# Attention and expert kernel on one core: third operands of the 320-column chunk dealt alike in all experts, attention steps handed out from a fixed list, three gate tiles

## The chip, the core and the metric

The kernel runs on one core of a Trainium2 chip. A core has five engines that run side by side, each working through its own queue in order: TensorE (PE in the profile; PEld are its weight loads), VectorE (DVE), ScalarE (ACT), GpSimd (POOL) and SyncE (SP), which here issues most of the transfers. They wait for each other by semaphores. Matmuls write to PSUM, the other operands lie in SBUF. The metric is the device time of one execution in microseconds (us). Three runs of the kernel before gave 425.80, 425.93 and 425.94, median 425.93.

## What is computed

Sketched attention gives `x`, and a mixture of four experts of width 1024 is applied to it, all in float32:

```python
a, b = x @ S1.T, x @ S2.T                    # phi(x): all 64 products a_i * b_j
kv, z = sum_s phi(k) v, sum_s phi(k)         # for each batch and head
x = (phi(q) @ kv) / (phi(q) @ z + 1e-6)      # 4 x 1088 rows of 4 * 32 = 128 columns
p = domain_probs / (domain_probs.sum(-1) + 1e-9)
out = sum over e of p[:, e] * (relu(x @ w1[e]) @ w2[e])    # e = 0..3, 128 -> 1024 -> 128
```

## The kernel before

The 4352 tokens lie along the columns and are cut into ten chunks (`CHUNKS`): 128, 448, six of 512, then 320 (chunk 8) and 384 (chunk 9). In each chunk but the first the four experts are worked through, each in eight blocks of 128 hidden units. A block is one slot of the main loop, 32 slots for each chunk. Attention for the later tokens is computed in between, in small steps from a generator (`pieces`).

A number is split into two or three parts of fewer bits, so that three fast passes of TensorE stand for one float32 product. A block has six matmuls, all recorded at L949:

- `h <- xs,wa` and `h <- xs,wb` when its slot opens (`opening`). ScalarE then scales h in place (`h <- h`, L1135).
- `h <- xs,wd` one slot later (`third`). Then the three operands of the second product are made from h: `ha`, the rounded high part of relu(h); `hb`, the rest (L1191, always VectorE); and `hc`, the operand of the third pass.
- `o <- ha,va` and `o <- hb,vb` five slots after the block opened (`LAG`, in `second`).
- `o <- hc,vd` only when the expert's eight blocks are through: ScalarE scales o (L1268), and `pay` hands the eight passes out over the next slots, 0, 1, 1, 2, 2, 2 (`DEALT`). Then the expert is gathered: VectorE multiplies o by the gate (L1396; L1394 for the first expert) and adds it to the total (L1397). The experts use two PSUM banks of o in turn, so the first o product of the next expert but one waits for this gather.

Who makes ha and hc is told by a letter for each block (`MAKERS`, a row of eight letters for each chunk and expert; the row of chunk 8 is the seventh). ScalarE's scaling of h and VectorE's hb are the same for all. The letters that matter here:

| letter | ScalarE | VectorE, besides hb | GpSimd |
|---|---|---|---|
| A | ha (L1184), hc (L1186) | - | hc = hb - hc (L1214) |
| P | ha | - | hc from ha (L1213), then L1214 |
| V | ha | hc from ha and hb (L1193) | - |
| D | hc | ha from h (L1188) | L1214 |
| N | ha, a "whole" from ha (L1197) | hc from h and the whole (L1206) | - |
| Z | ha | the whole (L1199), hc (L1206) | - |

L1193 has both operands in SBUF; L1188, L1191, L1199 and L1206 read h from PSUM. There are 7 tiles for ha, 6 for hb, 13 for hc, and six PSUM banks for h.

A gate is one expert's weight for each token of a chunk, repeated over all partitions: a tile of up to 512 columns, loaded by SyncE from a DRAM buffer (`load_gates`, L429). There are two tiles (`GATES`). The first two are loaded in slot 5, in front of the keys and values of batch 1 (`load_k(1)`, `load_v(1)`); each later one is issued behind a gather (`next_gates`) and takes the tile that this gather has just read. Loads that stand behind it in SyncE's queue wait with it.

How many attention steps follow a slot is decided while the program is built, by a planner: `on_vector` adds up an estimated time of what is issued to VectorE and ScalarE, `needed` and `left` say how many steps have to be done by when, and `work` hands out steps as credit and limits (`LIMIT`, `SLOT`, `LEAD`) allow. By the time of chunk 8 all but a few steps are done. In chunk 8 the other work besides the blocks is the gathers, the turning round of chunk 7's rows (L1362) and the splitting of chunk 9's tokens (`token_parts`: L886 on ScalarE, L891 on VectorE, L961 on GpSimd).

Of the kernel before, what the change touches and what calls it, by code (L numbers as in the profile page):

```python
# [24 lines left out]
def kernel(  # L25
# [24 lines left out]
    nc = tc.nc  # L50
# [4 lines left out]
    B, H, S, D = q.shape  # L55
# [10 lines left out]
    CW = 512  # L66
    GE = 160
    LAG = 5
    GATES = 2
    BUFFERS = (7, 6, 13)  # L70
    HA, HB, HC = BUFFERS
    WHOLE = 5
    MIXED = 16
    TURN = 1
    MAKER_1 = 'APXPDADA'
    MAKERS = (('APPVANAA', 'APAVPVAA', 'APPPAVAN', 'APVPAADA'), ('PAPPVBBA', 'APAVPAAA', 'APPVPANA', 'APVPADAA'), ('APPVNAAA', 'PAAVPAVA', 'AVPPPANA', 'APVPADAA'), ('APVAQNAA', 'APPVANPA', 'APVPAADA', 'APPVAAAD'), ('NPPVAPAN', 'APPAVAPA', 'NPPVAANP', 'APVPAADA'), ('APNVAPAA', 'APAPVAVA', 'APPVPANA', 'APVPDAAA'), ('APPVNAAZ', 'APAVVAAP', 'AAPVPPNA', 'APVPDAAA'), ('NVPVPAAV', 'PPVPVNPA', 'APVVPPDN', 'APvAAQaA'))
    TAIL = 4
    MAKER_TAIL = "PAVVXXTT"
    LAG_TAIL = 4
    DEALT_TAIL = (1, 1, 2)  # L80
    DEALT = (0, 1, 1, 2, 2, 2)
    LIMIT = 1300.0
    LIMIT_A = 1e9
    SLOT_A = 1500.0
    SLOT = 1600.0
    PLAIN = (2,)
    TOKENS_AT = 16
    AHEAD = 13
    TOKENS = 6
    LEAD = 6  # L90
    SETTLE = 1
    SPREAD = 2
    XD_BY = 'PPVVPPPVPP'
    Q_BY = 'PVPPPPVVPVVVPVVPPP'
    O_BY = 'AAAA'
    FETCH = 8
    HOLD = (3, 1)
    DELAY = 0
# [8 lines left out]
    UNITS = [[P, 448, 512], [576, 512], [576, 512], [576, 512]]  # L107

    CHUNKS = [P, 448] + [512] * 6 + [320, 384]
    NC = len(CHUNKS)  # L110
    START = [sum(CHUNKS[:m]) for m in range(NC + 1)]
# [34 lines left out]
    def load_k(b):  # L146
        kn[b] = lpool.tile([P, S], F32, tag="rows", name="kn")
        load_rows(k, b, kn[b])
# [266 lines left out]
    def parts(m):  # L415

        c, end, at = START[m], START[m] + CHUNKS[m], 0
        while c < end:
            n = min(end, (c // S + 1) * S) - c
            yield c // S, c % S, n, at  # L420
            c, at = c + n, at + n
# [3 lines left out]
    def load_gates(m, experts):  # L425
        for e in experts:
            gate[m, e] = mpool.tile([P, CW], F32, tag="gate", bufs=GATES, name="gate")
            for b, c, n, at in parts(m):
# [99 lines left out]
    def key_sum(b, p, kv, t0=0, n=NT):  # L528
        for t in range(t0, t0 + n):
            both(  # L530
                kv[:, 256 * p : 256 * p + 2 * (D + 1)],
                kps[b][:, t, p, :],
                vx[:, t, 2 * p : 2 * p + 2].rearrange("p h d -> p (h d)"),

                start=(p == t == 0),
                stop=(t == NT - 1),
                skip_group_check=True,
            )
# [275 lines left out]
    def queries_by_dram(b, c, n):  # L814

        for _ in range(FETCH):
            yield
# [7 lines left out]
        if c + n < S:  # L825
# [3 lines left out]
            if c + n + m == S and b < B - 1:  # L829
                load_k(b + 1)  # L830
        for _ in range(14 - FETCH):
            yield
# [133 lines left out]
    def start():  # L966
# [37 lines left out]
        for t0, n0 in ((0, 4), (4, 5)):  # L1004
            for p in range(2):
                key_sum(b, p, kv, t0, n0)
        qp = [xd_ for xd_ in (mpool.tile([P, CW], F32, tag="gate", bufs=GATES, name="qp") for _ in range(2))]
        for x in range(2):
# [40 lines left out]
    slots = [("pair", 0, e, f) for e in range(E) for f in range(NP)]  # L1049
    for m in range(1, NC):  # L1050
        slots += [("one" if m > 1 or FB * e + k >= MIXED else "mixed" if FB * e + k >= WHOLE else "whole", m, e, k) for e in range(E) for k in range(FB)]
    first_slot = {m: min(i for i, s in enumerate(slots) if s[1] == m) for m in range(NC)}
    per_chunk = {m: sum(s[1] == m for s in slots) for m in range(NC)}
# [23 lines left out]
    def final(m, e):  # L1077
        return m == NC - 1 and e == E - 1

    def letter(m, e, b):  # L1080
        if m == 1 and FB * e + b < MIXED:
            return "X"
        return (MAKER_TAIL if final(m, e) else MAKER_1 if m == 1 else MAKERS[m - 2][e])[b]

# [135 lines left out]
    def second(i):  # L1220
# [25 lines left out]
        elif kind == "one":  # L1246
# [19 lines left out]
            elif k == FB - 1:  # L1266
                if O_BY[e] == "A":
                    nc.scalar.activation(o[:, 0:n], o[:, 0:n], ACTF.Copy, scale=1.0 + R12)  # L1268
# [133 lines left out]
                yield  # L1402
            turn_back(m, total.pop(m)[:, 0:n])

    vector_time, scalar_time = [0.0], [0.0]

    def on_vector(inst):

        if inst.engine == mybir.EngineType.DVE and inst.outs:
            n = 1  # L1410
            for _, d in list(inst.outs[0].ap)[1:]:
                n *= d
            vector_time[0] += n / 0.96 + 80
        elif inst.engine == mybir.EngineType.Activation and inst.outs and type(inst).__name__ != "InstDMACopy":
            n = 1
            for _, d in list(inst.outs[0].ap)[1:]:
                n *= d
            scalar_time[0] += n * 0.834 + 50

    start()  # L1420
    nc.push_inst_callback(on_vector)
    pieces = front()
    done, credit = [0], [0]

    def piece():
        done[0] += 1
        next(pieces, None)


    needed, columns, count = [0] * NC, UNITS[0][0], 0  # L1430
    for b in range(B):
        count += 17 if b else 0
        for n in UNITS[b] if b else UNITS[0][1:]:
            count, columns = count + (20 if count else 18), columns + n
            for m in range(NC):
                if columns - n < START[m] + CHUNKS[m] <= columns:
                    needed[m] = count
    for i in range(3):
        begun_hp[i] = psum(ps_h, "h")
        half_columns(i, begun_hp[i], 0)  # L1440
# [25 lines left out]
        due.setdefault(first_slot[1] + HOLD[1] if held else i + (LAG_TAIL if final(*s[1:3]) else lag[s[0]]), []).append(i)  # L1466
    i = 0
    while i < len(slots) or i <= max(due) or owed:
        vector_time[0] = max(0.0, vector_time[0] - (SLOT * CHUNKS[slots[i][1]] / CW if i >= first_slot[1] and i < len(slots) else 900.0))
        scalar_time[0] = max(0.0, scalar_time[0] - (SLOT_A * CHUNKS[slots[i][1]] / CW if i >= first_slot[1] and i < len(slots) else 900.0))  # L1470
        if i < len(slots):
            kind, m, _, _ = slots[i]
            at = i - first_slot[m]
            while have[0] < START[m] + CHUNKS[m]:
                piece()

            gone = START[m] + CHUNKS[m] * at / per_chunk[m]
            left = lambda c: START[c] - (CHUNKS[c - 1] * AHEAD / per_chunk[c - 1] if c > 1 else 0) - gone
            rate = CHUNKS[m] / per_chunk[m] * max(
                [0] + [(needed[c] + (LEAD if c > 1 else 4) - done[0]) / left(c) for c in range(m + 1, NC) if left(c) > 0]  # L1480
            )

            def work(share):

                if not first_slot[1] <= i < first_slot[1] + 4:
                    credit[0] = min(credit[0] + rate * share, 3)
                while credit[0] >= 1 and vector_time[0] < LIMIT and scalar_time[0] < LIMIT_A:
                    credit[0] -= 1
                    piece()

            opening(i)
            if kind == "pair":
                work(0.5)
        for j in due.get(i, ()):
            second(j)
        if SETTLE:
            settle()
        third(i - DELAY if i < len(slots) else i)
        if not SETTLE:
            settle()  # L1500
        pay()
        next(ending, None)
        if i < len(slots):
            work(0.5 if kind == "pair" else 1)
            if at == per_chunk[m] - AHEAD and 0 < m < NC - 1:
                while have[0] < START[m + 1] + CHUNKS[m + 1]:
                    piece()
            for gen in to_part.get(i, ()):
                next(gen, None)
            if m == NC - 2 and at == per_chunk[m] // 2:  # L1510
                while have[0] < B * S:
                    piece()
                w2_tail = load_tail()
                one = dram.tile([P, P], F32, name="one")
                nc.sync.dma_start(one[:, :], unit[:, 0:P])
                nc.sync.dma_start(bass.AP(one.tensor, one.offset, [[P + 1, P], [1, 1]]), unit[:, P : P + 1])
                nc.sync.dma_start(unit[:, 0:P], one[:, :])
            if i == first_slot[1] + 10:
                for j in range(3):
                    load_plain(j)  # L1520
            for j in range(3, len(plain_order)):
                if i == first_slot[2] + 8 * (j - 3) + 7:
                    load_plain(j)
            if i == first_slot[4]:
                unit = cpool.tile([P, P + 1], F32, tag="dp", name="unit")
                nc.gpsimd.memset(unit[:, 0:P], 0.0)
                nc.gpsimd.memset(unit[:, P : P + 1], 1.0)
            if i == 2:
                gate_quotients()
            elif i == 5:  # L1530
                store_gates()
                next_gates(GATES)
                load_k(1)
                load_v(1)
        if i == 2:

            made_hp[3] = psum(ps_h, "h")
            for c in (0, HP):
                half_columns(3, made_hp[3], c)
        i += 1  # L1540
    for _ in ending:
        pass
    last_rows(NC - 1, unit)
    nc.pop_inst_callback()

# [1 line left out]
_INS = ["q", "k", "v", "S1", "S2", "moe_domain_probs", "moe_w1", "moe_w2"]  # L1547
# [26 lines left out]
```

## Time and profile before

| | |
|---|---|
| median of three runs | 425.93 us |
| the profiled execution's own time | 426.43 us |
| its span, first to last instruction | 424.7 us |
| instructions | 8812 |
| granted TensorE clock | 1.0 over the whole span |
| first product of chunk 8 (128x320) | 353.29 us |
| first product of chunk 9 (128x384) | 383.68 us |
| gathers of chunk 7 in this stretch, experts 2 and 3, begin at | 357.31 and 365.15 us |
| gathers of chunk 8, experts 0 to 2, begin at | 372.25, 379.64 and 387.52 us |

The profile is a trace of one execution, with a page that sums it up. In lines of groups a line names the line of the kernel, the engine, the operation, what it writes and reads with the shape, and how often; behind that stand busy time, the mean of one in ns, and the idle time of the engine before it with what ended it. In lines of the timeline the first two numbers are start and length in us, in tables of windows each engine's busy time in that stretch. Neighbouring instructions of one engine can overlap in the records: their lengths say more than an engine needs for each, and the distance from start to start in a full stretch is its real pace.

### The profile page before, as it was taken

How to read it: one execution, taken by the hardware profiler on the slowest of the kernel's cores; microseconds unless marked ns; L12 is line 12 of the kernel's file. 1: busy time of each engine (PE TensorE's matmuls, PEld its weight loads, DVE VectorE, ACT ScalarE, POOL GpSimd, SP SyncE). 2: the span in 40 equal slices, each digit the busy share in tenths (PEclk: the TensorE clock that was granted, in tenths of full speed). 3: DMA queues.
4: the chain of work that ended last, by engine and by line, in shares of the span. 5: the costliest groups of instructions: out<-in, count | busy, mean ns of one | idle time of the engine just before them, and what ended most of it. 6: DMA issues, size and time to landing. Idle time of an engine off the chain costs nothing.

```text
span 424.7 us, 8812 instructions
## 1 busy us (share of the span) xinstructions
PE 416.5 (98%) x2819; PEld 351.7 (83%) x2819; DVE 357.0 (84%) x626; ACT 382.0 (90%) x818; POOL 355.3 (84%) x371
## 2 busy tenths in 40 slices
PE   9999999999999999999999999999999999999996
PEld 7886677888888887878888887878778888989995
DVE  5869999888798896898799996896897878879894
ACT  4368898999999998999999988998999999999992
POOL 6441468999999999997999998897989999799992
PEclk9999999999999999999999999999999999999999
DMA  6925250446512401643602415212621221040110
GB/s 194 320 60 130 47 145 2 98 80 158 165 40 51 126 27 44 136 99 95 176 5 61 114 26 117 61 33 62 161 32 23 41 75 35 23 82 27 34 38 19
DMA packets 57646, 34.66 MB, mean 82 GB/s; under 512 B 34945, under 2 KB 50689, under 8 KB 57601
## 3 DMA queue, kind: packets, MB, share of 16 engines
q1 hardware_dynamic: 57504, 34.01, 31.5%
q8 instruction: 22, 0.36, 0.4%
q14 instruction: 24, 0.19, 0.2%
q10 hardware_dynamic: 96, 0.10, 0.1%
HBM read 28.94 MB, written 5.15 MB: 80 GB/s over the span
## 4 chain that ended last, share of the span: by engine, by line
PE 82%; ACT 8%; DVE 4%; issue 3%; DMA 2%; SPq 0%; DVEq 0%; ACTq 0%
PE o L949 36%; PE h L949 36%; PE h L318 6%; ACT ha L1184 3%; ACT h L1135 3%; ACT hc L1186 2%; PE h L497 1%; DMA qn_first<-in_q_dram 1%; PE o L318 1%; DMA kn<-in_k_dram 1%; PE h L1121 1%; DVE hb L1191 1%; DVE o L1396 1%; SPq L171 0%; DVE qs L637 0%
## 5 line engine op out<-in xcount | busy, mean ns | idle before, releaser
L1214 POOL TENSOR_TENSOR hc<-hb,hc 128x512 fp32r<-128x512 f32 (+3 forms) x204 | 252.5, 1260 | 23.1 <-DVE hb L1191 16.9
L1191 DVE SCALAR_TENSOR_TENSOR hb<-h,ha 128x512 fp32r<-128x512 f32 (+3 forms) x266 | 166.8, 641 | 48.9 <-ACT hc L1186 16.9
L1135 ACT ACTIVATE h<-h 128x512 f32<-128x512 f32 (+3 forms) x283 | 166.3, 588 | 4.1 <-PE h L949 3.5
L1184 ACT ACTIVATE ha<-h 128x512 fp32r<-128x512 f32 (+3 forms) x252 | 148.8, 590 | 2.0 <-PE h L949 0.4
L949 PE MATMUL h<-xs,wd 128*128 128x512 f32 (+3 forms) x283 | 109.2, 386 | 1.3 <-ACT h L1135 0.5
L949 PE MATMUL h<-xs,wa 128*128 128x512 f32 (+3 forms) x283 | 105.5, 373 | 0.0
L949 PE MATMUL h<-xs,wb 128*128 128x512 f32 (+3 forms) x283 | 102.5, 362 | 0.0
L949 PE MATMUL o<-ha,va 128*128 128x512 f32 (+3 forms) x266 | 96.8, 364 | 1.1 <-DVE total L1397 1.1
L949 PE MATMUL o<-hb,vb 128*128 128x512 f32 (+3 forms) x266 | 96.6, 363 | 0.0
L949 PE MATMUL o<-hc,vd 128*128 128x512 f32 (+3 forms) x262 | 79.7, 366 | 0.2
L1186 ACT ACTIVATE hc<-h 128x512 fp32r<-128x512 f32 (+3 forms) x124 | 74.1, 598 | 0.0
L949 PEld LDWEIGHTS h<-xs,wd 128*128 128x128 f32 x283 | 53.3, 188 | 19.8 <-ACT h L1135 11.6
L1213 POOL TENSOR_SCALAR hc<-ha 128x512 fp32r<-128x512 f32 (+3 forms) x80 | 57.4, 717 | 8.1 <-ACT ha L1184 1.6
L949 PEld LDWEIGHTS h<-xs,wa 128*128 128x128 f32 x283 | 53.5, 189 | 9.5 <-issue 2.9
L949 PEld LDWEIGHTS h<-xs,wb 128*128 128x128 f32 x283 | 53.5, 189 | 5.7 <-issue 0.6
L949 PEld LDWEIGHTS o<-ha,va 128*128 128x128 f32 x266 | 50.3, 189 | 7.5 <-PE h L949 2.3
L949 PEld LDWEIGHTS o<-hc,vd 128*128 128x128 f32 x262 | 48.5, 189 | 7.9 <-issue 1.6
L949 PEld LDWEIGHTS o<-hb,vb 128*128 128x128 f32 x266 | 50.3, 189 | 5.5 <-DVE hb L1191 0.2
L1193 DVE SCALAR_TENSOR_TENSOR hc<-ha,hb 128x512 fp32r<-128x512 f32 (+2 forms) x41 | 36.2, 882 | 1.4
L1268 ACT ACTIVATE o<-o 128x512 f32<-128x512 f32 (+3 forms) x33 | 18.4, 557 | 0.0
L1397 DVE TENSOR_TENSOR total<-o,total 128x512 f32<-128x512 f32 (+3 forms) x26 | 16.9, 650 | 0.9
L1396 DVE TENSOR_TENSOR o<-o,gate 128x512 f32<-128x512 f32 (+3 forms) x26 | 16.8, 647 | 0.3 <-PE o L949 0.3
(161 smaller groups left out, 405.2 us busy)
## 6 DMA issues: line engine op xcount, KB each, us to landing
w_sb<-in_moe_w_dram SPq DMA_DIRECT2D x8, 512.0 KB
gate<-gates SPq DMA_DIRECT2D x16, 256.0 KB
kn<-in_k_dram SPq DMA_DIRECT2D x4, 544.0 KB
gate<-gates SPq DMA_DIRECT2D x8, 224.0 KB
qs<-rows SPq DMA_DIRECT2D x6, 288.0 KB
qs<-rows SPq DMA_DIRECT2D x12, 144.0 KB
qn<-in_q_dram SPq DMA_DIRECT2D x3, 544.0 KB
vx<-in_v_dram SPq DMA_DIRECT2D x48, 32.0 KB
```

Source lines behind the costliest of these rows:

```text
L318: nc.tensor.matmul(out(s), weights(s), moving(s), **flags)
L949: nc.tensor.matmul(to, weights, t, **flags)
L1135: nc.scalar.activation(g, g, ACTF.Copy, scale=1.0 + R12)
L1184: nc.scalar.activation(ha, g, ACTF.Relu, scale=NEAR)
L1186: nc.scalar.activation(hc, g, ACTF.Relu, scale=NEAR * R12)
L1191: nc.vector.scalar_tensor_tensor(out=hb, in0=g, scalar=0.0, in1=high, op0=ALU.max, op1=ALU.subtract)
L1193: nc.vector.scalar_tensor_tensor(out=hc, in0=high, scalar=-R12, in1=rest, op0=ALU.mult, op1=ALU.add)
L1213: nc.gpsimd.tensor_scalar(out=hc, in0=high, scalar1=R12, scalar2=1.0, op0=ALU.mult, op1=ALU.mult)
L1214: nc.gpsimd.tensor_tensor(out=hc, in0=rest, in1=both_, op=ALU.subtract)
L1268: nc.scalar.activation(o[:, 0:n], o[:, 0:n], ACTF.Copy, scale=1.0 + R12)
L1396: nc.vector.tensor_tensor(out=o[:, 0:n], in0=o[:, 0:n], in1=g, op=ALU.mult)
L1397: nc.vector.tensor_tensor(out=total[m][:, 0:n], in0=o[:, 0:n], in1=total[m][:, 0:n], op=ALU.add)
```

## The change

Three things change. The numbers of attention steps that follow each slot are written down as digits (`PIECES`), and the planner goes. `GATES` is 3 instead of 2. And the four rows of letters of chunk 8 become one pattern, APVDAPVD, for all four experts; counted over its 32 blocks, A 14, P 9, V 5, N 2, Z 1, D 1 become A 8, P 8, V 8, D 8.

```diff
-    GATES = 2
+    GATES = 3
...
     MAKERS = (
...
-      ('APPVNAAZ', 'APAVVAAP', 'AAPVPPNA', 'APVPDAAA'),
+      ('APVDAPVD', 'APVDAPVD', 'APVDAPVD', 'APVDAPVD'),
...
-    LIMIT = 1300.0
-    LIMIT_A = 1e9
-    SLOT_A = 1500.0
-    SLOT = 1600.0
...
-    LEAD = 6
...
+    PIECES = "0110110111011000301101101110110100001212121212111122002211111021210221112102211121110111110003011102111110002111111111111100301111..."
...
-            def work(share):
-
-                if not first_slot[1] <= i < first_slot[1] + 4:
-                    credit[0] = min(credit[0] + rate * share, 3)
-                while credit[0] >= 1 and vector_time[0] < LIMIT and scalar_time[0] < LIMIT_A:
-                    credit[0] -= 1
+            def work():
+
+                steps[0] += 1
+                for _ in range(int(PIECES[steps[0] - 1])):
                     piece()
...
             if kind == "pair":
-                work(0.5)
+                work()
...
-            work(0.5 if kind == "pair" else 1)
+            work()
```

`on_vector`, `needed`, `gone`, `left` and `rate`, which only the planner used, are taken out with it.

More of the change, by code (lines that the diff above doesn't have):

```diff
@@ L75 @@
     MAKER_1 = 'APXPDADA'
-    MAKERS = (('APPVANAA', 'APAVPVAA', 'APPPAVAN', 'APVPAADA'), ('PAPPVBBA', 'APAVPAAA', 'APPVPANA', 'APVPADAA'), ('APPVNAAA', 'PAAVPAVA', 'AVPPPANA', 'APVPADAA'), ('APVAQNAA', 'APPVANPA', 'APVPAADA', 'APPVAAAD'), ('NPPVAPAN', 'APPAVAPA', 'NPPVAANP', 'APVPAADA'), ('APNVAPAA', 'APAPVAVA', 'APPVPANA', 'APVPDAAA'), ('APPVNAAZ', 'APAVVAAP', 'AAPVPPNA', 'APVPDAAA'), ('NVPVPAAV', 'PPVPVNPA', 'APVVPPDN', 'APvAAQaA'))
+    MAKERS = (('APPVANAA', 'APAVPVAA', 'APPPAVAN', 'APVPAADA'), ('PAPPVBBA', 'APAVPAAA', 'APPVPANA', 'APVPADAA'), ('APPVNAAA', 'PAAVPAVA', 'AVPPPANA', 'APVPADAA'), ('APVAQNAA', 'APPVANPA', 'APVPAADA', 'APPVAAAD'), ('NPPVAPAN', 'APPAVAPA', 'NPPVAANP', 'APVPAADA'), ('APNVAPAA', 'APAPVAVA', 'APPVPANA', 'APVPDAAA'), ('APVDAPVD', 'APVDAPVD', 'APVDAPVD', 'APVDAPVD'), ('NVPVPAAV', 'PPVPVNPA', 'APVVPPDN', 'APvAAQaA'))
     TAIL = 4
@@ L95 @@
     O_BY = 'AAAA'
+    PIECES = "01101101110110003011011011101101000012121212121111220022111110212102211121022111211101111100030111021111100021111111111111003011110210211100301111021111110012111100210211002111111020111100121111021101110030111101201011000210110020101100201010100000000000000000000000000000000000000000000000000000000000000000000000000000"
     FETCH = 8
@@ L1403, in gather @@
             turn_back(m, total.pop(m)[:, 0:n])
[L1405 to L1418, printed above, removed]
     start()
-    nc.push_inst_callback(on_vector)
     pieces = front()
-    done, credit = [0], [0]
+    steps = [0]
     def piece():
-        done[0] += 1
         next(pieces, None)
[L1430 to L1437, printed above, removed]
     for i in range(3):
@@ L1468 @@
     while i < len(slots) or i <= max(due) or owed:
-        vector_time[0] = max(0.0, vector_time[0] - (SLOT * CHUNKS[slots[i][1]] / CW if i >= first_slot[1] and i < len(slots) else 900.0))
-        scalar_time[0] = max(0.0, scalar_time[0] - (SLOT_A * CHUNKS[slots[i][1]] / CW if i >= first_slot[1] and i < len(slots) else 900.0))
         if i < len(slots):
@@ L1475 @@
                 piece()
[L1477 to L1481, printed above, removed]
-            def work(share):
-                if not first_slot[1] <= i < first_slot[1] + 4:
-                    credit[0] = min(credit[0] + rate * share, 3)
-                while credit[0] >= 1 and vector_time[0] < LIMIT and scalar_time[0] < LIMIT_A:
-                    credit[0] -= 1
+            def work():
+                steps[0] += 1
+                for _ in range(int(PIECES[steps[0] - 1])):
                     piece()
@@ L1543 @@
     last_rows(NC - 1, unit)
-    nc.pop_inst_callback()
 _INS = ["q", "k", "v", "S1", "S2", "moe_domain_probs", "moe_w1", "moe_w2"]
```

## The prediction

> **What bounds the kernel now.** I read the page first: busy shares, then the chain that ended last.
>
> ```profile
> PE 416.5 (98%) x2819; PEld 351.7 (83%) x2819; DVE 357.0 (84%) x626; ACT 382.0 (90%) x818; POOL 355.3 (84%) x371
> ...
> PE 82%; ACT 8%; DVE 4%; issue 3%; DMA 2%; SPq 0%; DVEq 0%; ACTq 0%
> ```
>
> TensorE sets the end; the others can only cost the time in which it waits for them. So I went to the stage that the change touches. The chunk of 320 columns issues its first product at 353.29 and the last chunk (384 columns) starts at 383.68, so the stage is 30.4 us. I then took the busy time of each engine from 358.64 (the first hb behind the gather of chunk 7, expert 2) to 388.45 (the first VectorE instruction behind the gather of chunk 8, expert 2).
>
> ```profile
> 358.64:388.45 29.81, 29.12 (x192) 26.97 (x191) 25.47 (x53) 29.61 (x84) 25.91 (x34) 1.00 0.21 46
> ...
> 388.00:400.00 12.00, 12.00 (x77) 11.72 (x76) 11.41 (x23) 11.90 (x31) 10.92 (x13) 1.00 0.14 40
> ```
>
> After the length come PE, PEld, DVE, ACT, POOL. ScalarE is full (29.61 of 29.81), VectorE has 4.34 us free. (The second row, from the last chunk, is used below.) The busy time of PE hides its waits, so I read these from the starts of its matmuls:
>
> ```profile
> 366.08 0.30 PE L949 MATMUL h<-xs,wb 128*128 128x320 f32 x1
> 366.71 0.37 PE L949 MATMUL o<-ha,va 128*128 128x320 f32 x1 [0.33 <-DVE total L1397]
> ...
> 380.17 0.30 PE L949 MATMUL o<-hb,vb 128*128 128x320 f32 x1
> 380.61 0.40 PE L949 MATMUL h<-xs,wd 128*128 128x320 f32 x1
> ```
>
> Undisturbed 320-wide matmuls start 0.1355 us apart (360.46, 360.60, 360.74, 360.87); 366.08 to 366.71 is 0.63, so 0.49 is lost, and 380.17 to 380.61 loses 0.30. Summed over every start from 358.56 to 389.58 (steps 0.1355, 0.1625 and 0.2155 for 320, 384 and 512 columns), the gaps of 0.07 or more lose 3.04 us. Of this 0.25 lies at 358.87, behind a gather in front of which nothing changes, and 0.10 at 389.34, past the stretch. **At most 2.7 us can be had.** Apart from the 0.57 at 366.71, behind a VectorE gather, nearly all are at wd products waiting for ScalarE's h (L1135), or at hc products while ScalarE scales o (L1268). VectorE waits too:
>
> ```profile
> DVE hb L1191 <- ACT ha L1184: 1.2, 4, 0.6
> DVE hb L1191 <- PE h L949: 1.1, 2, 0.6
> DVE hb L1191 <- ACT hc L1186: 0.9, 2, 0.5
> DVE hb L1191 <- PE o L949: 0.6, 1, 0.6
> DVE hb L1191 <- POOL hc L1214: 0.2, 1, 0.2
> ```
>
> 4.0 us in all: idle because ScalarE, and TensorE behind it, were late.
>
> **The change, part by part.** *PIECES* holds the very counts that the planner arrives at in the kernel before, and the planner runs at build time. The order of TensorE's instructions is the same in both kernels, that of the others differs only in the chunk of 320 and, on SyncE, in the gate loads. Cost nothing.
>
> *GATES 3* puts one more gate load (224 KB) in front of the keys of batch 1 on SyncE: a gate issue takes 0.43 us (two took 0.86 at 33.08), the key load went out at 33.99 and is first read at 52.97, so 18.5 us hide it; without that cover it would cost its 0.43. Every later gate load still stands behind the gather whose tile it takes, so the loads queued behind it wait as before. No VectorE wait on a gate load is in the list of waits, so nothing is to be had either: zero, bounds 0 and 0.4. Each then brings the gate of one expert later than before, so gates come a whole expert sooner; the tightest was issued at 379.01 and used at 387.52, 8.5 us ahead.
>
> *Letters.* The 32 blocks of the chunk go from A14 P9 V5 N2 Z1 D1 to A8 P8 V8 D8. ScalarE: 7 ha and 2 "whole" fewer, one hc more, so 8 of its 80 block instructions go. Start to start in a full stretch (362.20 to 362.51, 361.88 to 362.20) hc costs 0.31 and ha 0.32; a whole waits for its own ha and costs 0.54. 6 x 0.32 + 2 x 0.54 = 3.0 us. 29.61 - 3.0 = 26.6, and TensorE without its waits would need 29.8 - 2.7 = 27.1: ScalarE stops being the limit, by little. GpSimd: one TENSOR_SCALAR less (0.54), the same 24 TENSOR_TENSOR; the first expert has six instead of five (+0.84), hidden since the first hc pass comes 13 slots after its block opens (361.1 made, 367.19 used); if that cover failed it is late by that 0.84.
>
> VectorE pays: V from 5 to 8, ha in D from 1 to 8, three hc of N and Z and one Z whole fewer.
>
> ```profile
> L1191 DVE SCALAR_TENSOR_TENSOR hb<-h,ha 128x320 fp32r<-128x320 f32 x31 | 14.4, 484 | 3.8 <-PE h L949 1.1 <-ACT ha L1184 1.0 <-ACT hc L1186 0.9
> L1193 DVE SCALAR_TENSOR_TENSOR hc<-ha,hb 128x320 fp32r<-128x320 f32 x5 | 3.6, 723 | 0.2
> ...
> L1188 DVE TENSOR_SCALAR ha<-h 128x320 fp32r<-128x320 f32 x1 | 0.5, 475 | 0.0
> ```
>
> Start to start: hb 0.41 (four in 1.73 at 384.52), ha 0.51 (384.01 to 384.52). The five hc of V took 0.41, 0.69, 0.41, 0.60 and 1.10 to the next start, mean 0.64, and the hb ahead of each 0.10 more than usual: 0.74. N's hc 0.41, Z's whole 0.52. So 3 x 0.74 + 7 x 0.51 - 3 x 0.41 - 0.52 = **+4.0 us on VectorE**, as much as the waits that it had.
>
> **The sum.** VectorE's queue is in order: behind a late V stand the next ha and hb (o products wait for both) and the gathers, and behind a gather the first o product of the next expert but one. The tightest is the gather of chunk 8, expert 2: it ends at 388.53 and TensorE takes its bank at 388.82; a hand-off took 0.14 at 366.71, so 0.15 is spare. If VectorE never idles it does the stretch in 25.5 + 4.0 = 29.5, plus the 0.3 of idle time that is no listed wait, 29.8: as before. By start-to-start prices alone its work was 31 hb 12.7, one 384-wide hb 0.5, five V 3.7, four hc of N and Z 1.7, a whole and an ha 1.0, four gathers 1.33 + 0.54 + 0.93 + 0.93, the turn of chunk 7's rows 0.62 and a token part 1.03: 25.0; it becomes 29.0, which is 0.8 sooner. TensorE gains the difference and the spare 0.15: between 0.15 and 0.95 us. I take 0.5, the middle, since both ends come from the same rows. The 2.2 that remain of 2.7 turn from waits for ScalarE into waits for VectorE. From 390 on TensorE runs full (the second row above), so the 0.5 reaches the end. On the profiled execution (426.43; span 424.7 and 1.73 around it) that is 425.9; its median stands 0.5 lower, 425.93, and so the forecast is **425.4**, own range 425.0 to 425.9. A measurement here tells 0.2%, 0.85 us, from no change, so this is no change.
>
> **What the hc of V really costs** decides more than anything else. The row first:
>
> ```profile
> 369.59 0.49 DVE L1193 SCALAR_TENSOR_TENSOR hc<-ha,hb 128x320 fp32r<-128x320 f32 x1
> ...
> 382.51 1.18 DVE L1193 SCALAR_TENSOR_TENSOR hc<-ha,hb 128x320 fp32r<-128x320 f32 x1
> ```
>
> At 369.59 GpSimd was idle; at 382.51 its TENSOR_TENSOR had begun 0.03 earlier and ran 0.86. hb, which reads h from PSUM, is steady at 0.484. So 0.41 and 1.10 are the bounds of one such step. The Trainium skill ("SBUF — State Buffer", section "SBUF: two separate sides") speaks against the change: a VectorE instruction with two SBUF inputs and a GpSimd one lock a shared port pair for a whole instruction, and the later one stands still. This trace agrees (1.18 is about the rest of 0.83 plus 0.35). A lock met at random would make the average hc dearer than the five rows do. By that the sum would be the second rival's, 426.6.
>
> **Rivals.** (1) *VectorE keeps up.* The regular deal puts hc into GpSimd's gaps and it costs 0.41 + 0.10 each: 8 x (0.74 - 0.51) = 1.8 us less, gain 0.5 + 1.8 = 2.3 of the possible 2.7: **423.6**. For: two of five cost 0.41, and VectorE ran 11.41 of 12.00 in 388 to 400 with no TensorE wait. Against: GpSimd is busy 25.9 of 29.8. (2) *Slower: GpSimd holds VectorE up.* GpSimd's four instructions per four blocks are three of 0.87 and one of 0.46; caught at random, the rest of one is (3 x 0.87 x 0.87 + 0.46 x 0.46) / (2 x 3.07) = 0.40, times the 95% that it is busy, 0.38; hc is 0.41 + 0.38 + 0.10 = 0.89 instead of 0.74, and 8 x 0.15 = 1.2 us late. That alone takes the 0.5 and 0.7 more, **426.6**; if all were caught as at 382.51 (1.20), 8 x 0.46 = 3.7 gives 429.1. It decides from 0.80 per V on. For: the two 384-wide ones at 389.03 and 390.74 lasted 0.74 and 1.07. Against: the five measured. (3) *It doesn't do what it says:* ScalarE is freed but the waits at 366.71 and at bank hand-overs stay put, as they are VectorE's: **425.9**.
>
> **Chances.** Forecast 0.34, rival 1 0.31, rival 2 0.25, rival 3 0.10. Faster by over 0.2%: rival 1 and the edge of the forecast, 0.33. Slower: rival 2, 0.25. Within: 0.42. The range takes in rival 1 and rival 2 at its first price: 423.6 to 427.0.
>
> **What would show it.** ScalarE's busy share in the stage drops by 3 us and PEld's waits for h L1135 vanish there; VectorE's share rises above 28 of the stage with hardly a wait for ScalarE; new TensorE waits name DVE total L1393 or hb. L1193's row (now L1189), x8 at 320: mean near 0.72 confirms the sum, under 0.6 rival 1, over 0.85 rival 2. The first 353 us must be the same to 0.2 us; if they are not, PIECES or GATES was priced wrongly, and so was the forecast.

## The result and the profile after

| | before | after |
|---|---|---|
| median of five runs each, same chip | 425.93 us | 427.78 us (427.64 to 428.20) |
| ratio, 95% interval | 1 | 1.0043 (1.0031 to 1.0055) |
| the profiled execution's own time, span | 426.43, 424.7 us | 427.78, 426.0 us |
| first product of chunk 8 to that of chunk 9 | 30.39 us | 30.84 us |
| first product of chunk 8 to that of the last block | 61.35 us | 62.71 us |

The change costs 1.85 us of the median; the forecast was a gain of 0.5. Here and below, ratios and intervals are estimated from the fast runs alone (one of the twelve runs of e10, 1101.73 us, is not in them), so a ratio can differ from the quotient of the two medians, by up to 0.0009. Lines behind the constants are four lower in the changed kernel (hb L1187, V's hc L1189, ha of D L1184, the gather L1392 and L1393).

The page of the changed kernel, busy time by engine and the chain that ended last:

```profile
PE 416.1 (98%) x2819; PEld 351.0 (82%) x2819; DVE 362.1 (85%) x632; ACT 380.4 (89%) x810; POOL 354.4 (83%) x370
...
PE 85%; ACT 5%; DVE 3%; issue 2%; DMA 2%; SPq 0%; ACTq 0%; DVEq 0%
```

TensorE does the same 2819 matmuls and still ends last; VectorE has 5.1 us more to do, ScalarE 1.6 less. The next rows are the stretch between the same two VectorE instructions as in the prediction (first hb behind the gather of chunk 7, expert 2, to the first behind that of chunk 8, expert 2) and 388 to 400, with the busy time of PE, PEld, DVE, ACT, POOL:

```profile
358.34:389.73 31.39, 30.09 (x194) 27.31 (x192) 29.82 (x60) 28.64 (x79) 27.29 (x35) 1.00 0.18 45
388.00:400.00 12.00, 11.49 (x72) 11.18 (x72) 11.57 (x23) 11.54 (x30) 9.41 (x12) 1.00 0.14 33
```

The stretch is 31.39 us instead of 29.81. ScalarE, which had 0.20 us free in it, now has 2.75. VectorE's 29.82 busy are what its whole old stretch lasted. And from 388 to 400, where TensorE had been full, it now idles for half a microsecond. Which engine waits for which from 358.34 to 390.20 (us in all, times, longest):

```profile
PE o L945 <- DVE total L1393: 0.9, 2, 0.5
...
DVE hb L1187 <- DVE ha L1184: 0.5, 1, 0.5
PE o L945 <- DVE hb L1187: 0.4, 2, 0.2
PEld h L945 <- ACT h L1131: 0.4, 1, 0.4
```

VectorE's one listed wait is for an ha of its own; of the 4.0 us before, 2.1 were for ScalarE and 1.7 for TensorE. TensorE now waits for VectorE's gather (total L1393) and for its hb, as the starts of its matmuls show:

```profile
365.67 0.30 PE L945 MATMUL h<-xs,wb 128*128 128x320 f32 x1
366.36 0.37 PE L945 MATMUL o<-ha,va 128*128 128x320 f32 x1 [0.39 <-DVE total L1393]
...
369.30 0.40 PE L945 MATMUL o<-ha,va 128*128 128x320 f32 x1
369.90 0.40 PE L945 MATMUL o<-hb,vb 128*128 128x320 f32 x1 [0.19 <-DVE hb L1187]
...
384.23 0.40 PE L945 MATMUL o<-ha,va 128*128 128x320 f32 x1
384.82 0.40 PE L945 MATMUL o<-hb,vb 128*128 128x320 f32 x1 [0.19 <-DVE hb L1187]
...
389.12 0.33 PE L945 MATMUL h<-xs,wb 128*128 128x384 f32 x1
389.96 0.40 PE L945 MATMUL o<-ha,va 128*128 128x384 f32 x1 [0.51 <-DVE total L1393]
```

Start to start less the undisturbed step (0.1355, or 0.1625 behind a 384-wide one), these four lose 0.55, 0.46, 0.45 and 0.68 us. Summed so over all starts from 352 to 404, TensorE loses 4.57 us in the changed kernel and 3.26 in the one before: 1.31 more, which is the 1.36 between the first product of chunk 8 and that of the last block, but for rounding. The rest of the two profiled executions' difference lies outside these two chunks: chunk 8 begins 0.30 earlier, the transfer out at the end takes 0.24 longer.

The groups of the stage name the instruction:

```profile
L1189 DVE SCALAR_TENSOR_TENSOR hc<-ha,hb 128x320 fp32r<-128x320 f32 x8 | 7.9, 988 | 0.3
...
L1209 POOL TENSOR_SCALAR hc<-ha 128x320 fp32r<-128x320 f32 x8 | 4.6, 574 | 0.7
...
L1184 DVE TENSOR_SCALAR ha<-h 128x320 fp32r<-128x320 f32 x8 | 3.8, 474 | 0.0
```

The mean of V's hc is 988 ns, against 723 before, and over the 850 that the prediction set as the mark of its second rival. The ha of D is as long as in the one case before (474 and 475 ns). From the start of each hc to the next VectorE start it is 0.89, 0.96, 1.13, 0.88, 0.57, 0.88, 1.10 and 0.88 us, mean 0.91, where the five before had 0.64.

### The profile page after: what moved, and what is told of

It is laid out like the page before. It is cut to its first block, busy times and chain, and to the rows that moved or that the text cites. A ratio compares the mean times of both kernels' runs of the same rounds, so it can differ in the third digit from the quotient of the medians.

```text
span 426.0 us, 8812 instructions
## 1 busy us (share of the span) xinstructions
PE 416.1 (98%) x2819; PEld 351.0 (82%) x2819; DVE 362.1 (85%) x632; ACT 380.4 (89%) x810; POOL 354.4 (83%) x370
## 4 chain that ended last, share of the span: by engine, by line
PE 85%; ACT 5%; DVE 3%; issue 2%; DMA 2%; SPq 0%; ACTq 0%; DVEq 0%
PE o L945 37%; PE h L945 36%; PE h L314 7%; ACT h L1131 2%; ACT ha L1180 2%; PE o L314 2%; PE h L493 1%; DMA qn_first<-in_q_dram 1%; DVE hb L1187 1%; DMA kn<-in_k_dram 1%; PE h L1117 1%; ACT hc L1182 1%; DVE o L1392 1%; SPq L167 0%; PE h L1339 0%
## 5 line engine op out<-in xcount | busy, mean ns | idle before, releaser
L1187 DVE SCALAR_TENSOR_TENSOR hb<-h,ha 128x512 fp32r<-128x512 f32 (+3 forms) x266 | 165.8, 641 | 45.0 <-ACT hc L1182 14.4
L1131 ACT ACTIVATE h<-h 128x512 f32<-128x512 f32 (+3 forms) x283 | 166.2, 587 | 5.1 <-PE h L945 4.1
L1180 ACT ACTIVATE ha<-h 128x512 fp32r<-128x512 f32 (+3 forms) x245 | 145.5, 594 | 2.5 <-PE h L945 0.9
L1209 POOL TENSOR_SCALAR hc<-ha 128x512 fp32r<-128x512 f32 (+3 forms) x79 | 56.0, 709 | 8.1 <-ACT ha L1180 1.8
L1189 DVE SCALAR_TENSOR_TENSOR hc<-ha,hb 128x512 fp32r<-128x512 f32 (+2 forms) x44 | 41.1, 933 | 1.5
L1393 DVE TENSOR_TENSOR total<-o,total 128x512 f32<-128x512 f32 (+3 forms) x26 | 16.9, 651 | 0.9
L1392 DVE TENSOR_TENSOR o<-o,gate 128x512 f32<-128x512 f32 (+3 forms) x26 | 16.8, 647 | 0.3 <-PE o L945 0.3
```

Of the source, the lines that this page charges most:

```text
L1131: nc.scalar.activation(g, g, ACTF.Copy, scale=1.0 + R12)
L1180: nc.scalar.activation(ha, g, ACTF.Relu, scale=NEAR)
L1187: nc.vector.scalar_tensor_tensor(out=hb, in0=g, scalar=0.0, in1=high, op0=ALU.max, op1=ALU.subtract)
L1189: nc.vector.scalar_tensor_tensor(out=hc, in0=high, scalar=-R12, in1=rest, op0=ALU.mult, op1=ALU.add)
L1209: nc.gpsimd.tensor_scalar(out=hc, in0=high, scalar1=R12, scalar2=1.0, op0=ALU.mult, op1=ALU.mult)
L1392: nc.vector.tensor_tensor(out=o[:, 0:n], in0=o[:, 0:n], in1=g, op=ALU.mult)
```

## Experiments

Medians are compared with runs of the kernel before on the same chip, so the ratio is what counts from one table row to another. The "price of V" is the mean, in the profiled execution, from the start of V's hc in chunk 8 to VectorE's next start (none is given where V is another instruction or VectorE idles behind it). The stage columns are from that one execution too, which need not be a typical one (those of e2, e2b, e7 and e8 were the fastest of their runs); they are, as above, from the first product of chunk 8 to that of chunk 9 and to that of the last block.

| run | letters of chunk 8, gates | median / before | ratio (95%) | to chunk 9 | to the last block | price of V |
|---|---|---|---|---|---|---|
| before | old, 2 | 425.93 | 1 | 30.39 | 61.35 | 0.64 |
| after | APVDAPVD, 3 | 427.78 / 425.93 | 1.0043 (1.0031, 1.0055) | 30.84 | 62.71 | 0.91 |
| e0_changed_again | the same | 428.01 / 426.30 | 1.0031 (1.0018, 1.0045) | 30.15 | 62.02 | 0.82 |
| e1_old_letters | old, 3 | 426.17 / 426.11 | 1.0004 (0.9994, 1.0014) | 30.40 | 61.36 | 0.64 |
| e2_two_gates | APVDAPVD, 2 | 427.10 / 426.11 | 1.0023 (1.0014, 1.0032) | 30.82 | 62.41 | 0.91 |
| e2b_two_gates_again | the same | 427.18 / 426.30 | 1.0016 (1.0001, 1.0030) | 30.13 | 61.76 | 0.82 |
| e3_no_d | APVAAPVA, 3 | 427.62 / 426.30 | 1.0027 (1.0014, 1.0040) | 30.89 | 62.68 | - |
| e4_psum_hc | V from h in PSUM, 3 | 426.71 / 426.11 | 1.0022 (1.0011, 1.0032) | 29.86 | 61.61 | - |
| e5_no_pool_tt | no TENSOR_TENSOR on GpSimd, 3 | 425.28 / 426.11 | 0.9981 (0.9972, 0.9989) | 29.80 | 60.42 | 0.50 |
| e6_old_plus_d | old, four A to D, 3 | 426.71 / 426.30 | 1.0008 (0.9993, 1.0023) | 30.00 | 61.46 | 0.48 |
| e7_d_before_v | APDVAPDV, 3 | 426.55 / 426.28 | 1.0007 (0.9998, 1.0015) | 29.93 | 61.16 | 0.74 |
| e8_v_second | AVPDAVPD, 3 | 426.10 / 426.28 | 0.9994 (0.9983, 1.0004) | 30.15 | 60.86 | 0.70 |
| e8b_v_second_again | the same | 425.50 / 426.01 | 0.9990 (0.9981, 0.9998) | 30.10 | 60.82 | 0.69 |
| e11_v_second_two_gates | AVPDAVPD, 2 | 425.72 / 426.01 | 0.9993 (0.9984, 1.0002) | 30.08 | 60.79 | 0.74 |
| e9_z_for_v | APZDAPZD, 3 | 426.91 / 426.28 | 1.0015 (1.0003, 1.0028) | 30.34 | 61.71 | - |
| e10_z_half_d | APZDAPZA, 3 | 427.02 / 426.28 | 1.0021 (1.0010, 1.0032) | 30.25 | 62.05 | - |

### Which of the three edits it is

e1_old_letters is the changed kernel with the old seventh row, e2_two_gates the changed kernel with the old number of gate tiles:

```diff
-      ('APVDAPVD', 'APVDAPVD', 'APVDAPVD', 'APVDAPVD'),     # e1
+      ('APPVNAAZ', 'APAVVAAP', 'AAPVPPNA', 'APVPDAAA'),
...
-    GATES = 3                                              # e2
+    GATES = 2
```

> The changed kernel with the old letters in the chunk of 320, so only the fixed list and the third gate tile are left of the change. Theory (GpSimd holds up the hc of V on VectorE, which has become the limit; all of it is due to the letters): as before, 425.9, within 0.4. Rival (the third gate tile or the fixed list costs the time, through transfers or places in memory): 427.4 to 427.8.

> The changed kernel with two gate tiles, so fixed list and new letters. Theory: as the changed kernel, 427.8, within 0.4. Rival (the third gate tile costs): 425.9 to 426.3.

With the old letters the time of before is back (1.0004) and so are its stage lengths, to 0.01 us: the list of attention steps and the third gate tile cost nothing there, and the letters are the change. With the new letters two tiles came out 0.7 us under three, so e2 missed its 427.8 within 0.4. A second pair on another chip was to say whether that is real:

> The changed kernel once more, beside the next ones on the same chip, as their measure: 1.003 to 1.0055 of the kernel before; from the first product of the chunk of 320 to the last block's first product 62.4 to 62.8 us, against 61.35 before.

> The changed kernel with two gate tiles, repeated beside the changed kernel, since it came out at 1.0023 on its own. Theory (letters alone): the same as the changed kernel within 0.4 us. Rival (the third gate tile costs some of it): 0.6 to 1.0 us less.

Again 0.8 us between the medians, where the rival had 0.6 to 1.0, but with overlapping intervals (1.0018 to 1.0045 and 1.0001 to 1.0030). The repeated changed kernel has the ratio that was expected of it, but its way to the last block, 62.02, lies under the expected 62.4 to 62.8; why is shown further down. Of the 0.8 us the stages show 0.26 to 0.30 us, most of it at one wait for hb near 384, 0.45 us long with three tiles and 0.25 with two. Why the third tile should do that isn't known; with another pattern of letters (e11, below) it does nothing.

### Does GpSimd hold V's hc up

e4_psum_hc makes V's hc in chunk 8 from h in PSUM and hb, so that one operand only lies in SBUF. It leaves out the right third operand of these eight blocks. e5_no_pool_tt takes GpSimd's TENSOR_TENSOR out of chunk 8 and leaves out the subtraction in 24 blocks.

```diff
# e4, in chunk 8
-  nc.vector.scalar_tensor_tensor(out=hc, in0=high, scalar=-R12, in1=rest, op0=ALU.mult, op1=ALU.add)
+  nc.vector.scalar_tensor_tensor(out=hc, in0=g, scalar=0.0, in1=rest, op0=ALU.max, op1=ALU.subtract)
# e5, in chunk 8
-  nc.gpsimd.tensor_tensor(out=hc, in0=rest, in1=both_, op=ALU.subtract)
```

> The changed kernel; in the chunk of 320 the hc of V is taken from h in PSUM and hb instead of from ha and hb in SBUF: one instruction of the same kind and size with one operand in SBUF instead of two. It leaves out the right third operand of these eight blocks. Theory: hc drops from 0.99 to about 0.49 with GpSimd as busy as before, VectorE does the stretch of 31.4 us in about 31.4 - 8 x 0.5 = 27.4, and TensorE's waits for it nearly vanish: 423.7 to 424.8. Rival (it is the number of VectorE instructions, the eight ha of D above all, not their length): hc stays above 0.85 or the time stays at 427.2 to 427.8.

> The changed kernel without GpSimd's TENSOR_TENSOR in the chunk of 320 (24 of them), so the third operand of A, P and D lacks hb there. Theory: nothing to stand behind but the eight short TENSOR_SCALAR, so the hc of V, still from two operands in SBUF, drops to 0.5 to 0.6 and the time to 423.5 to 424.8, as with hc from PSUM. Rival (number of VectorE instructions): hc stays above 0.85 or 427.2 to 427.8. Rival (an hc with two operands in SBUF is slow by itself at this rate): hc stays near 0.99 here, while it drops with one in PSUM.

The group of V's hc in chunk 8 with h from PSUM, GpSimd as busy as before:

```profile
L1190 DVE SCALAR_TENSOR_TENSOR hc<-h,hb 128x320 fp32r<-128x320 f32 x8 | 3.9, 491 | 0.3
```

and with two operands in SBUF, but without GpSimd's TENSOR_TENSOR:

```profile
L1189 DVE SCALAR_TENSOR_TENSOR hc<-ha,hb 128x320 fp32r<-128x320 f32 x8 | 4.5, 568 | 0.6
```

Either way the half microsecond is gone; in e5 six of the eight last 0.49. Of the other two the long one (0.93) met the one TENSOR_TENSOR left, that of the token splitting, and the other (0.66, at 359.13) a TENSOR_SCALAR with one operand, from 359.00 to 359.46. So neither the operands nor GpSimd's work alone makes V's hc dear, only both at once. e5 is the first version faster than before (0.9981). The 423.5 to 424.8 expected were too low by half a microsecond. Of its 0.93 us up to the last block, 0.59 are won before chunk 9, and nothing is given back behind it.

e4 missed by 2 us. It has the shortest way to chunk 9 but one (29.86) and loses all of it again in chunk 9, at two gathers. Its timeline shows where:

```profile
393.11 1.36 DVE L1192 SCALAR_TENSOR_TENSOR hc<-ha,hb 128x384 fp32r<-128x384 f32 x1
...
395.27 0.33 PE L945 MATMUL h<-xs,wb 128*128 128x384 f32 x1
...
395.37 0.49 DVE L1396 TENSOR_TENSOR total<-o,total 128x320 f32<-128x320 f32 x1
...
396.01 0.40 PE L945 MATMUL o<-ha,va 128*128 128x384 f32 x1 [0.42 <-DVE total L1396]
...
396.76 1.00 POOL L1213 TENSOR_TENSOR hc<-hb,hc 128x384 fp32r<-128x384 f32 x1
396.83 1.35 DVE L1192 SCALAR_TENSOR_TENSOR hc<-ha,hb 128x384 fp32r<-128x384 f32 x1
...
412.04 0.40 PE L945 MATMUL o<-ha,va 128*128 128x384 f32 x1 [0.40 <-DVE total L1396]
```

Chunk 9 has V of its own, untouched by any of this. In the kernel before the two at 394.24 and 397.18 lasted 0.58 and 0.62; here they last 1.36 and 1.35, since each begins just behind a TENSOR_TENSOR of 1.00 (the second 0.07 behind the one at 396.76), the gather of chunk 8's last expert behind the first is late, and TensorE waits 0.58 us (395.27 to 396.01 less 0.1625). At 412.04 it loses another 0.56 at the next gather (0.07 in the kernel before): the last instruction of that gather begins at 411.33, in the kernel before at 411.34, so a TensorE that arrives earlier only waits longer for it.

### Does it matter where among GpSimd's work V falls

First by accident. The changed kernel and its second measurement are the same program, and their profiles differ by 0.69 us in the way to chunk 9 (30.84 and 30.15). The timelines of VectorE and GpSimd around the third V, changed kernel:

```profile
367.04 0.87 POOL L1210 TENSOR_TENSOR hc<-hb,hc 128x320 fp32r<-128x320 f32 x1
367.05 1.21 DVE L1189 SCALAR_TENSOR_TENSOR hc<-ha,hb 128x320 fp32r<-128x320 f32 x1
...
368.18 0.70 DVE L1358 STREAM_TRANSPOSE ob<-total 128x512 f32<-128x512 f32 x1
```

and its second measurement:

```profile
367.07 1.22 POOL L1210 TENSOR_TENSOR hc<-hb,hc 128x320 fp32r<-128x320 f32 x1
367.07 0.49 DVE L1189 SCALAR_TENSOR_TENSOR hc<-ha,hb 128x320 fp32r<-128x320 f32 x1
367.48 0.70 DVE L1358 STREAM_TRANSPOSE ob<-total 128x512 f32<-128x512 f32 x1
```

The two start together to a hundredth. Where GpSimd is first, its TENSOR_TENSOR lasts 0.87 and hc 1.21; where VectorE is first, hc lasts 0.49 and the TENSOR_TENSOR 1.22. In the first case TensorE then loses 0.27 and 0.46 us at 369.30 and 369.90, in the second nothing there. The two profiles with two gate tiles fall apart in the same way (hc 1.20 with a loss of 0.71 us, and 0.49 with none).

Then on purpose: the same counts of letters, V in another place.

```diff
-      ('APVDAPVD', 'APVDAPVD', 'APVDAPVD', 'APVDAPVD'),
+      ('APDVAPDV', 'APDVAPDV', 'APDVAPDV', 'APDVAPDV'),     # e7
+      ('AVPDAVPD', 'AVPDAVPD', 'AVPDAVPD', 'AVPDAVPD'),     # e8, e8b, e11
```

> The changed kernel with V and D changed over (APDVAPDV in all four experts), so the counts of letters and all instructions are the same, only the place of V's hc among GpSimd's work differs. Theory (the lock, and the phase between VectorE and GpSimd): the price of V's hc moves with the place, anywhere from 0.5 to 1.2 us mean, and the time with it: under 0.75 us mean it is at most 426.6, over 0.9 at least 427.2. Rival (the counts alone set the time, as the sum of instructions would have it): mean 0.95 to 1.0 us and 427.8 +- 0.4, whatever the place.

> The changed kernel with P and V of each first half changed over (AVPDAVPD in all four experts), the counts the same. Theory (phase): as for APDVAPDV, the mean of V's hc may be anything from 0.5 to 1.2 us, and the stage from the first product of chunk 8 to that of chunk 9 goes with it: 30.4 us or less where the mean is under 0.75, 30.8 or more where it is over 0.95. Rival (counts alone): mean 0.95 to 1.0 us, 427.8 +- 0.4.

Both take away what the change lost: 1.0007 and 0.9994. The price of V goes down to 0.74 and 0.70 and its duration to 0.79 and 0.78 us, between the two marks that were set, so the marks for either side are missed, but the rival, 0.95 to 1.0 us and 427.8 whatever the place, is out by more than a microsecond. To see whether it lasts, and what the third tile does here:

> AVPDAVPD with three tiles once more, beside the kernel with two. Theory (the place of V's hc among GpSimd's work sets the price): the mean of V's hc is 0.7 to 0.85 us again and the ratio to before 0.998 to 1.001. Rival (the first measurement was a lucky one): a mean over 0.9 us, ratio 1.002 or more, as in the changed kernel.

> AVPDAVPD in all four experts with two gate tiles instead of three. With the changed kernel's own pattern two tiles measured 0.0015 to 0.0020 of the time less (0.6 to 0.8 us), twice. Theory (the third tile costs by itself): the same here, 0.6 to 0.8 us less than AVPDAVPD with three tiles, 425.3 to 425.6 where before has 426.1 to 426.3. Rival (the third tile costs nothing; the difference came from where the hc of V fell among GpSimd's work): within 0.3 us of AVPDAVPD with three tiles, either way.

The group in the second measurement of AVPDAVPD:

```profile
L1189 DVE SCALAR_TENSOR_TENSOR hc<-ha,hb 128x320 fp32r<-128x320 f32 x8 | 6.1, 765 | 0.3
...
L1209 POOL TENSOR_SCALAR hc<-ha 128x320 fp32r<-128x320 f32 x8 | 3.9, 488 | 0.7
```

It lasts: 0.9990 (0.9981 to 0.9998). Four of its eight hc last 0.51 to 0.60 us and four 0.76 to 1.17; in the changed kernel one lasted 0.64 and seven 0.95 to 1.21. GpSimd's TENSOR_SCALAR is back from 574 to 488 ns. Two tiles or three are within 0.22 us of each other, so with these letters the third costs nothing. This is the best complete version that was run; it beats the changed kernel by 0.4 to 0.5% and the one before by 0.1%, at the edge of what can be told.

### Without D, with more D, without the lock

e3_no_d turns the eight D back into A, e6_old_plus_d keeps the old letters with four A made D (`APPVNADZ`, `APDVVADP`, `ADPVPPNA`, `APVPDADA`).

> The changed kernel with D undone (APVAAPVA in the chunk of 320): ScalarE makes those ha again. Theory: VectorE loses 8 x 0.58 = 4.6 us and is no longer late, ScalarE gains 2.6 us and is as full as before, so its waits come back: from the first product of the chunk to the last block's 60.9 to 61.8, 425.5 to 426.5. Rival (hc of V alone decides, the ha of D cost nothing): hc of V stays near 1.0 us and the time at that of the changed kernel.

> The changed kernel with the old letters of the chunk of 320, but four of their A made D (APPVNADZ APDVVADP ADPVPPNA APVPDADA): no V more, 4 x 0.55 = 2.2 us of the 4 that VectorE had free, 4 x 0.32 = 1.3 us off ScalarE. Theory: ScalarE's waits shrink and VectorE doesn't become the limit: 60.3 to 61.2 from the first product of the chunk to the last block's, 0.2 to 1.0 us less than before. Rival (any ha on VectorE costs, as the eight of D do): more than 61.6, slower than before.

e3 missed: 427.62 instead of 425.5 to 426.5, although V's hc fell to a mean of 657 ns. ScalarE is full again (30.20 of 30.40 us from 352.9 to 383.3, as before the change), TensorE loses 0.1 to 0.3 at many wd and hc products, so that it reaches chunk 9 half a microsecond later than before the change; behind the gathers in chunk 9 it loses another 0.58 at 396.94 and 0.57 at 412.97. Taking the D out gains nothing: they are what frees ScalarE. e6 missed too: no difference instead of a gain. It is 0.39 faster to chunk 9, its V fall well (0.48), and it gives 0.50 back at 396.94, where the V ahead of the gather in chunk 9 (394.13) lasts 1.27 instead of 0.58.

Z makes hc in two VectorE instructions that both read h from PSUM. e9_z_for_v puts it in V's place, e10_z_half_d also turns every second D back:

```diff
+      ('APZDAPZD', 'APZDAPZD', 'APZDAPZD', 'APZDAPZD'),     # e9
+      ('APZDAPZA', 'APZDAPZA', 'APZDAPZA', 'APZDAPZA'),     # e10
```

> The changed kernel with Z in place of V (APZDAPZD): hc is made from the whole and from h in PSUM, two instructions of VectorE instead of one, and none of them has two operands in SBUF. Theory (the lock): no instruction of VectorE is held up by a TENSOR_TENSOR of GpSimd, so both rows stay within 0.46 to 0.56 us mean; a Z then costs 0.41 + 0.52 = 0.93 us against the 1.01 measured for V, 8 x 0.08 = 0.6 us less VectorE work in the stage, and GpSimd, which is not held either, comes out of chunk 8 without a backlog: 426.3 to 427.4. Rival (VectorE simply has too many instructions, whatever their operands): eight more of about 0.45 us, 3.6 us more VectorE work, 429 or more.

> As with Z in place of V, and one of the two D of each row turned back into A (APZDAPZA: A 12, P 8, Z 8, D 4). VectorE has 4 x 0.51 = 2.0 us less work than with APZDAPZD, ScalarE 4 x 0.32 = 1.3 us more (28 of 30.4 us in the stage, still below the kernel before). Theory (VectorE is what TensorE waits for, and without the lock its work can be summed): faster than APZDAPZD by 0.5 to 1.5 us, 425.2 to 426.5. Rival (ScalarE is what matters, so fewer of its instructions are better): slower than APZDAPZD, with waits for h back at the wd products.

The two instructions of Z, and GpSimd's TENSOR_SCALAR, in e9:

```profile
L1202 DVE SCALAR_TENSOR_TENSOR hc<-h,hid 128x320 fp32r<-128x320 f32 x8 | 3.9, 492 | 0.6
...
L1209 POOL TENSOR_SCALAR hc<-ha 128x320 fp32r<-128x320 f32 x8 | 3.8, 481 | 0.7
...
L1195 DVE SCALAR_TENSOR_TENSOR hid<-ha,h 128x320 f32<-128x320 f32 x8 | 3.8, 477 | 0.0
```

None is held up, and e9's 426.91 lies in the 426.3 to 427.4 expected: eight instructions more on VectorE, and a ratio of 1.0015 against the 1.0031 and 1.0043 of the changed kernel, though its interval overlaps that of the 1.0031. It is no gain over before, since a Z (0.55 and 0.41, start to start) costs 0.96 us, more than a V that falls well. e10 missed: it was to be 0.5 to 1.5 faster than e9 and is the same. It has lost the wait for the gather near 389 (0.66 in e9) and got one of 0.59 at 396.51, again behind a V of chunk 9 of 1.36 us, and one of 0.56 at 412.54.

## Why the prediction was wrong

**What bounds the kernel: right.** TensorE ended last, and nothing but its waits in and behind chunk 8 made the difference.

**PIECES and GATES at nothing: right for the old letters** (1.0004 with both), and for AVPDAVPD. Chunk 8 began 0.30 us earlier, over the 0.2 that the prediction allowed, but the two profiles of AVPDAVPD with three tiles differ by 0.41 there (352.68 and 353.09), so 0.30 says nothing about an edit. With the change's own letters the third tile may cost up to 0.8 us; that is open.

**ScalarE freed, waits for h gone: right.** 2.75 us of the stretch are free instead of 0.20, and of the waits for L1135 (now L1131) in the stage one is left.

**The price of V: the step that failed.** "0.64, and the hb ahead of each 0.10 more than usual: 0.74" was taken from five hc that stood, with other letters, in other places of GpSimd's work. The eight of the change cost 0.91 + 0.10 = 1.01. That is 8 x 0.27 = 2.2 us. A smaller miss is ha in D: from its start to that of its hb 0.55 to 0.58 instead of 0.51 in seven of eight cases, and 0.93, with the one listed wait in it, in the eighth, together 5.0 instead of 4.1. The token part (0.61 instead of 1.03) and the first gather of chunk 8 (0.40 instead of 0.54) give 0.6 back. With the prediction's 29.0 that is 29.0 + 2.2 + 0.9 - 0.6 = 31.5 us of VectorE, and the stretch was 31.39: VectorE set its length, as the sum had it, but its work was mis-sized.

**The sum itself holds where its price holds.** With AVPDAVPD the price is 0.69 + 0.10 = 0.79, near the 0.74 assumed, and the median is 0.5 us under before (425.50 to 426.01; 0.2 in the first measurement). The forecast was 0.5; that the second measurement meets it to a tenth is luck, as the two differ by 0.3. The counts in it were right; it took one number as the property of an instruction that is the property of its place.

**Rival 2, "GpSimd holds VectorE's hc up", is what happened.** It was to decide "from 0.80 per V on"; the price was 1.01, and its own arithmetic then gives 2.2 less 0.5, 1.7 us slower, against 1.85 between the medians and 1.35 between the two profiled executions. Its 426.6 was too low because it let hc be "caught at random" (0.89). Even that was not what a random catch costs by the traces. GpSimd's busy share in its own row is 87% (25.9 of 29.8), not 95%. And all eight hc of the changed kernel end 0.35 us behind the GpSimd instruction that they met; alone one takes 0.49, so a rest of r costs r - 0.14, not r. An estimate from these numbers is (3 x 0.73 x 0.73 + 0.32 x 0.32) / (2 x 3.07) x 0.87 = 0.24, which makes 0.75 per V, as good as the 0.74 of the forecast. So the lock alone doesn't explain 1.01; the phase does. V's hc began 0.01 to 0.28 us behind the start of a TENSOR_TENSOR in seven of eight cases, four of them 0.25 to 0.28, and was held up by 0.4 us or more in all seven. What ties the two engines together so closely isn't shown. The Trainium skill ("SBUF — State Buffer", section "SBUF: two separate sides") has a VectorE instruction with two SBUF inputs and a GpSimd instruction that reads SBUF take a shared port pair whole, first come first served. The runs agree on all three points: 0.49 us with one operand in PSUM, 0.49 without GpSimd's TENSOR_TENSOR, and either one as the loser by a hundredth of a microsecond (1.21 or 1.22).

**Rival 1, hc in GpSimd's gaps, did not come about**: with the counts of the change no pattern that was run got below 0.69 with GpSimd's work in place, and in e5, without it, the price was 0.50.

**"From 390 on TensorE runs full, so the 0.5 reaches the end": right for losses only.** The 1.3 us lost up to 390 reached the end. But what e4, e6 and e10 had gained by the start of chunk 9 (0.53, 0.39 and 0.14), TensorE lost again near 396, by 0.50 to 0.59 us, behind V of chunk 9 that met GpSimd, and e4 and e10 lost another 0.56 at 412; e3 lost as much there with nothing gained. TensorE's full row in the kernel before was a row of its own phase. It isn't the early arrival alone: e5, e7 and e8 came early too (0.59, 0.46 and 0.24) and lost nothing near 396. What decides isn't shown.

## What to carry to other kernels

An instruction that shares a lock with another engine has no price of its own: before giving it more places, look at what the other engine is doing at each new place, start to start, and ask whether a regular pattern will meet it every time. Where such a row is the largest term of a sum, try the same counts in another order before judging the idea: here AVPDAVPD instead of APVDAPVD turned +0.4% into -0.1%. And a stage that ran without waits after yours did so at one phase; time won ahead of it can be lost in it, as in e4.

## What was not expected of the hardware

Of two instructions of 0.49 us and 0.87 us that start within 0.01 us of each other on VectorE and GpSimd, V's hc as the loser ends 0.35 us after the winner, GpSimd's TENSOR_TENSOR as the loser lasts 0.35 us longer, and which one loses differs between profiles of one program: a single such case goes with 0.7 us of the 428. GpSimd's TENSOR_SCALAR, with one operand, is longer too (574 ns in the changed kernel, 481 in e9, where no V ran in chunk 8).
